# An attention and two expert layers: k's positions over 128 partitions for each head, and another order of the head

## The chip, the cores and the metric

One Trainium2 chip, one core. The metric is the device time of one execution in microseconds; the time of a kernel is the median of its runs.

## The reference

q, k and v are (4, 8, 576, 64): batch, heads, positions, width. q is made a softmax over its last axis, k a softmax over the *positions*; then `kv = k_s^T v` (64 by 64 for each head) and `attn = q_s kv`. The heads are laid side by side, which gives 2304 tokens of width 512. Two expert layers follow, each `x @ w_in` (512 to 2048), an activation (softplus in the first, ELU in the second) and `@ w_out` (2048 to 512):

```python
k_s = np.exp(k - np.max(k, axis=2, keepdims=True))
k_s = k_s / (np.sum(k_s, axis=2, keepdims=True) + 1e-09)
kv = np.einsum('bhsd,bhse->bhde', k_s, v)
x = np.einsum('bhsd,bhde->bhse', q_s, kv)   # then heads side by side, 2304 x 512
x = softplus(x @ w_in) @ w_out
x = elu(x @ w2_in) @ w2_out
```

## The kernel before, in words

The tokens are cut into six blocks of 384 (`t` = 0 to 5), worked on in three pairs. Each expert layer goes over the pairs, and for each pair over eight slices of 256 hidden columns ("quads"): the upward product (L833, with a seven-product scheme on halves; L895 in plain float32 for the first two quads of the first layer), the activation, the downward product (L1040, L1045, L1007, L1185). Weights arrive as raw words, are turned into float32 by ScalarE and VectorE (`add_words`, L662 to L687) and written back for later use.

**The head** is what runs before and beside the first of these. For q, `add_q` loads 384 rows, takes the softmax (VectorE, POOL or VectorE, ScalarE), transposes (L506), multiplies with the block-diagonal `kvbd` (L522) and copies the result to `sx` (L535), which is the input of the first layer. For k and v, `add_k(t, b, hps)` does one batch `b` and one or two pairs of heads `hps`: for batch 0 one pair in each of four steps, for batches 1, 2 and 3 two pairs in each of two steps. A pair puts head 0 on partitions 0 to 63 and head 1 on 64 to 127; each partition has nine positions of its head. In `add_k`, in order:

- L309 loads k, one DMA a pair, and L328 (batch 0, through `vr`, copied at L332) or L337 loads v, both on SP's queue. v has a column of ones beside it, for the sums.
- L346: VectorE takes the maximum over the nine positions of each partition, in four instructions.
- L354: TensorE transposes these maxima; L358: VectorE reduces them over a head's partitions.
- L366: TensorE spreads the maxima to the partitions, one matmul a head, into `pb`.
- L373: VectorE subtracts `pb` from k; L381: ScalarE takes exp.
- L390: TensorE adds up `kv` and the sums over positions into `pk`: for each of nine positions, two matmuls of 64 rows, one for each head, in two tiles of 64x64 of the array.
- L399, L403, L414 or L416: the sums become reciprocals, and the scaled `kv` goes into `kvbd`.

**What sets the order.** Every piece of work is a step with an engine, a cost, what it reads and writes, and for matmuls of the layers a due time. `Plan.order` (L59) works back from the due times to a latest start for each step, and then plays the engines forward: among the steps that can start at about the same time, the one with the earliest latest start goes first. A group of steps can be called more urgent by a number in `PRI` (L1366), which is taken off its latest starts: `k00` is the k steps of the first block that begin with pair 0, `q00` the q steps of the same, `k10` and `k12` those of the second block, `i0` and `o0` the words of the first slices of `w_in` and `w_out`, and so on. The order that comes out is written into the program once; each engine, and SP's queue of DMAs, works through its list in that order.

```python
@step(DMA, n * t_dma(P * C * D * 4), make=[...], after=LAT, behind=behind)          # k, L300
@step(DMA, t_dma(P * C * D * 4), make=[(vr, "xf")], after=LAT, behind=[kload[...]]) # v of batch 0, L325
@step(PE, 1.45 * n, r=[kk, vk], make=[(pk, bank(t))])                               # L383
def t_dma(n): return max(0.5, n / 300e3)                                            # LAT is 3.0 us
```

Of the kernel before, what the change touches and what calls it, by code (L numbers as in the profile page):

```python
# [8 lines left out]
F32 = mybir.dt.float32  # L9
# [3 lines left out]
ALU = mybir.AluOpType  # L13
AX = mybir.AxisListType

PE, ACT, DVE, POOL, DMA = "PE", "ACT", "DVE", "POOL", "DMA"
# [134 lines left out]
def t_dve(n, fast=False):  # L151
    return 0.069 + n / (1920 if fast else 960)
# [6 lines left out]
def t_dma(n):  # L159
    return max(0.5, n / 300e3)  # L160
# [3 lines left out]
def attention_moe_moe_kernel(  # L164
# [30 lines left out]
    nc = tc.nc  # L195
    B, H, S, D = q.shape
    NT, DM = out.shape
    DFF = w1_in.shape[1]
    P = 128
# [5 lines left out]
    NPAIR = NB // 2  # L205
    NP = H // 2
    C = S // 64
    EPS = 1e-9

    def pool(name, space=None, bufs=1):  # L210
# [8 lines left out]
        "g": (2, [P, 2 * BLK], F32), "gh": (3, [P, 2 * BLK], F32R), "gl": (3, [P, 2 * BLK], F32R),  # L219
        "s": (4, [P, BLK], F32), "xq": (2, [P, BLK], F32), "y": (2, [P, DM], F32), "yl": (2, [P, DM], F32),  # L220
        "k": (1, [P, 2 * C * D], F32), "v": (1, [P, 2 * C * (D + 1)], F32), "q": (1, [P, 2 * BLK], F32),
        "mx": (2, [P, 2 * D], F32), "mt": (1, [P, 8 * D], F32), "m": (4, [2 * D, 2], F32),
        "rs": (4, [P, 2], F32), "qm": (4, [P, 4 * R, 1], F32), "qd": (4, [P, 4 * R, 1], F32),
    }
    banks = {"ha": 2, "acc0": R, "acc1": R}
# [6 lines left out]
    T = {}  # L232

    def new(key, dt=None):
        ring = plan.tile_ring[key]
        _, shape, ring_dt = rings.get(ring, (0, [P, 512], F32))
        T[key] = pools[ring].tile(shape, dt or ring_dt, tag=ring, name="_".join(str(x) for x in key))
        return T[key]
# [28 lines left out]
    start, beside, now = {}, {}, 45.0  # L267
# [19 lines left out]
    def bank(t, rows=False):  # L287

        return "ha" if t > 1 else "acc0" if rows and not t else "acc1"

    def add_k(t, b, hps, behind=()):

        kk, vk, mx, pt, pb, pk, rs, m = (
            (s, b, hps[0]) for s in ("k", "v", "mx", "pt", "pb", "pk", "rs", "m")
        )
        n = len(hps)
        early = t == 0
        kt = lambda: T[kk][:, : n * C * D].rearrange("p (g c d) -> p g c d", g=n, d=D)
        vt = lambda: T[vk][:, : n * C * (D + 1)].rearrange("p (g c d) -> p g c d", g=n, d=D + 1)

        @step(
            DMA, n * t_dma(P * C * D * 4), make=[(kk, EARLY[0][hps[0]] if early else "k"), (vk, EARLY[1][hps[0]] if early else "v")],
            after=LAT, behind=behind,
        )
        def _():
            new(vk, F32)
            new(kk, F32)
            for g, hp in enumerate(hps):
                nc.sync.dma_start(  # L309
                    out=kt()[:, g],  # L310
                    in_=k[b, 2 * hp : 2 * hp + 2].rearrange("h (p c) d -> (h p) c d", c=C),
                )

        for hp in hps:
            kload[b, hp] = _

        @step(POOL, 0.05 * n, w=[vk])
        def _():
            nc.gpsimd.memset(vt()[:, :, :, D : D + 1], 1.0)

        vsrc = lambda hp: v[b, 2 * hp : 2 * hp + 2].rearrange("h (p c) d -> (h p) c d", c=C)
        if early:
            vr = ("vr", b, hps[0])

            @step(DMA, t_dma(P * C * D * 4), make=[(vr, "xf")], after=LAT, behind=[kload[b, hps[0]]])  # L325
            def _():
                T[vr] = new(vr, F32)[:, : C * D].rearrange("p (c d) -> p c d", c=C)
                nc.sync.dma_start(out=T[vr], in_=vsrc(hps[0]))  # L328

            @step(ACT, t_act(C * D), r=[vr], w=[vk])  # L330
            def _():
                nc.scalar.copy(vt()[:, 0, :, :D], T[vr])  # L332
        else:
            @step(DMA, n * t_dma(2 * P * C * D * 4), w=[vk], after=LAT)
            def _():
                for g, hp in enumerate(hps):
                    nc.sync.dma_start(out=vt()[:, g, :, :D], in_=vsrc(hp))  # L337

        mt = ("mt", b, hps[0])

        @step(DVE, sum(t_dve(n * x * D) for x in (4, 2, 1, 1)), r=[kk], make=[(mx, "mx"), (mt, "mt")])
        def _():
            half = new(mt)[:, : 4 * n * D].rearrange("p (g c d) -> p g c d", g=n, d=D)
            top = lambda o, x, y: nc.vector.tensor_tensor(o, x, y, op=ALU.max)  # L346
            top(half, kt()[:, :, :4], kt()[:, :, 4:8])
            top(half[:, :, :2], half[:, :, :2], half[:, :, 2:])
            top(half[:, :, 0], half[:, :, 0], half[:, :, 1])
            top(new(mx)[:, : n * D].rearrange("p (g d) -> p g d", g=n), half[:, :, 0], kt()[:, :, 8])  # L350

        @step(PE, 0.11, r=[mx], make=[(pt, bank(t))])
        def _():
            nc.tensor.transpose(new(pt)[: n * D, :P], T[mx][:, : n * D], ident)  # L354

        @step(DVE, t_dve(128), r=[pt], make=[(m, "m")])
        def _():
            nc.vector.tensor_reduce(  # L358
                new(m)[: n * D], T[pt][: n * D, :P].rearrange("d (h p) -> d h p", h=2), axis=AX.X, op=ALU.max
            )  # L360

        @step(PE, 0.12 * n, r=[m], make=[(pb, bank(t))])
        def _():
            p = new(pb)
            for j in range(2):
                nc.tensor.matmul(  # L366
                    p[64 * j : 64 * j + 64, : n * D], T[m][: n * D, j : j + 1].to_broadcast([n * D, 64]),
                    ident[: n * D, : n * D], start=True, stop=True,
                )

        @step(DVE, t_dve(n * C * D), r=[pb], w=[kk])
        def _():
            nc.vector.tensor_tensor(  # L373
                kt(), kt(),
                T[pb][:, : n * D].rearrange("p (g o d) -> p g o d", g=n, o=1).to_broadcast([P, n, C, D]),
                op=ALU.subtract,
            )

        @step(ACT, t_act(n * C * D), w=[kk], tab="exp")
        def _():  # L380
            nc.scalar.activation(kt(), kt(), AF.Exp)  # L381

        @step(PE, 1.45 * n, r=[kk, vk], make=[(pk, bank(t))])  # L383
        def _():
            p = new(pk)
            for g in range(n):
                for c in range(C):
                    for j in range(2):
                        rows = slice(64 * j, 64 * j + 64)
                        nc.tensor.matmul(  # L390
                            p[rows, g * (D + 1) : (g + 1) * (D + 1)], kt()[rows, g, c, :], vt()[rows, g, c, :],
                            start=(c == 0), stop=(c == C - 1),
                        )

        pkv = lambda: T[pk][:, : n * (D + 1)].rearrange("p (g d) -> p g d", g=n)

        @step(DVE, 0.07, r=[pk], make=[(rs, "rs")])
        def _():
            nc.vector.tensor_scalar(new(rs)[:, :n], pkv()[:, :, D], EPS, None, op0=ALU.add)  # L399

        @step(DVE, 0.075, w=[rs])
        def _():
            nc.vector.reciprocal(T[rs][:, :n], T[rs][:, :n])  # L403

        eng = DVE if early else ACT

        @step(eng, (0.28 if early else 0.5) * n, r=[pk, rs], w=[("kvbd", b % 2, hp) for hp in hps])
        def _():
            for g, hp in enumerate(hps):
                for j in range(2):  # L410
                    rows = slice(64 * j, 64 * j + 64)
                    o, i, f = kvbd[b % 2, hp][rows, rows], pkv()[rows, g, :D], T[rs][rows, g : g + 1]
                    if eng == DVE:
                        nc.vector.tensor_scalar(o, i, f, None, op0=ALU.mult)  # L414
                    else:
                        nc.scalar.activation(o, i, AF.Copy, scale=f)  # L416
# [868 lines left out]
    def add_store(m, p):  # L1285
# [55 lines left out]


    PRI = dict(
        k00=97, q00=38, k01=54, q01=13, k02=167, q02=154, k03=94, q03=54, k10=9, q10=83, k12=24, q12=11,
        k20=157, q20=11, k22=95, q22=30, k30=136, q30=45, k32=30, q32=0, x00=6, x01=36, x02=32, x10=48, x11=48,
        x12=213, y=59, w=-34, ahead=148, i0=-2, i1=43, i2=48, i3=173, i4=-23, i5=52, i6=66, i7=17, o0=105,
        o1=26, o2=29, o3=-28, o4=45, o5=18, o6=-2, o7=10,
    )

    def early(kind):  # L1350
# [23 lines left out]
    ahead = [(0, 1, 2), (0, 1, 4), (0, 1, 6), *((0, 2, f) for f in (0, 2, 3, 5, 6))]  # L1374
# [91 lines left out]
```

## Time and profile before

| | |
|---|---|
| median of 3 runs | 832.95 us (832.44 to 833.37) |
| the profiled execution, its own time | 833.62 us |
| its span, first to last instruction | 831.9 us, 13270 instructions |
| TensorE busy | 809.3 us, 97% |
| VectorE busy | 657.5 us, 79% |
| ScalarE busy | 564.7 us, 68% |
| DMA | 205.33 MB, mean 247 GB/s |

How to read it: a busy share is an average over the span, and the head and the layers have different limits. A matmul of float32 shows as two records. Lines are those of the kernel before; a group of instructions is named by what it writes and reads, with the shapes in partitions x elements.

### The profile page before, as it was taken

The page shows a single profiled execution, that of the slowest core. Times are in us where ns is not written, and L with a number is a line of the kernel's source. Part 1 is how long each engine was busy: PE and PEld are TensorE (multiplying, and loading weights), DVE is VectorE, ACT ScalarE, POOL GpSimd, SP SyncE. Part 2 cuts the span into 40 slices and gives each one's busy share as a digit, 9 for nine tenths or more (in the row PEclk, how much of TensorE's full clock was granted, in tenths as well). Part 3 has the DMA queues.
Part 4 walks back from the last instruction along what each step waited for, and adds up shares of the span by engine and source line. Part 5 has one row for each costly group of instructions (what it writes and reads, how often), then busy time and mean ns, then how long its engine had stood idle before and what let it go on. Part 6 is the DMA issues. An engine that isn't in the chain of part 4 may idle for free.

```text
span 831.9 us, 13270 instructions
## 1 busy us (share of the span) xinstructions
PE 809.3 (97%) x5110; PEld 732.4 (88%) x5110; DVE 657.5 (79%) x1088; ACT 564.7 (68%) x889; POOL 6.1 (1%) x28
## 2 busy tenths in 40 slices
PE   5799999999999999999999999999999999999997
PEld 4455788888889999999999998898999999999997
DVE  7879999979887768777679788968468697766775
ACT  4878987876787856756657767667466675557552
POOL 2000000000000000000000000000000000000000
PEclk9999999999999999999999999999999999999999
DMA  9597786636985556576855898987687676787563
GB/s 288 155 284 234 225 283 197 196 115 206 284 263 215 181 206 236 206 253 221 321 191 218 289 371 331 328 325 242 239 311 292 234 284 222 271 278 301 202 225 147
DMA packets 75166, 205.33 MB, mean 247 GB/s; under 512 B 18784, under 2 KB 34144, under 8 KB 65632
## 3 DMA queue, kind: packets, MB, share of 16 engines
q1 hardware_dynamic: 75104, 204.49, 71.0%
q8 instruction: 40, 0.66, 0.3%
q14 instruction: 22, 0.18, 0.1%
HBM read 143.65 MB, written 60.82 MB: 246 GB/s over the span
## 4 chain that ended last, share of the span: by engine, by line
PE 82%; DVE 8%; ACT 5%; DMA 2%; issue 2%; DVEq 0%; ACTq 0%; SPq 0%
PE ub L833 21%; PE acc L1007 15%; PE acc L1045 13%; PE uc L833 11%; PE Pb L1185 8%; PE ua L833 5%; PE Pc L1185 4%; PE Pa L1185 2%; PE px L522 1%; DMA wf_i<-wfd 1%; DVE mt L346 1%; PE acc L1040 1%; PE pk L390 1%; DMA raw_i<-in_moe_w_in_dram 1%; PE pq L506 1%
## 5 line engine op out<-in xcount | busy, mean ns | idle before, releaser
L833 PE MATMUL ub<-xf,wf_i 128*128 128x384 f32 x1104 | 226.5, 339 | 1.4 <-ACT s L846 1.1
L833 PEld LDWEIGHTS ub<-xf,wf_i 128*128 128x128 f32 x1104 | 189.3, 188 | 13.4 <-ACT s L846 4.3
L846 ACT COPY s<-ub 128x384 f32<-128x384 f32 x138 | 65.8, 477 | 72.7 <-PE ub L833 71.6
L833 PE MATMUL uc<-xf,wf_i 128*128 128x384 f32 x552 | 111.8, 337 | 0.7 <-ACT g L916 0.7
L1007 PE MATMUL acc<-gh,wo_o 128*128 128x512 f32 (+1 forms) x512 | 111.7, 340 | 0.0
L1045 PE MATMUL acc<-wo_o,gh 128*128 128x512 f32 x336 | 106.7, 398 | 0.0
L833 PEld LDWEIGHTS uc<-xf,wf_i 128*128 128x128 f32 x552 | 95.1, 188 | 5.7 <-ACT g L916 1.9
L867 DVE TENSOR_TENSOR h<-uc,s 128x384 f32<-128x384 f32 x92 | 51.1, 555 | 52.6 <-PE uc L833 47.5
L1007 PEld LDWEIGHTS acc<-gh,wo_o 128*128 128x128 f32 x512 | 82.9, 188 | 7.3
L1045 PEld LDWEIGHTS acc<-wo_o,gh 128*128 128x128 f32 x336 | 61.4, 188 | 9.0 <-ACT yt L1295 0.2
L1045 PE MATMUL acc<-wo_o,gl 128*128 128x512 f32 x168 | 66.5, 396 | 0.0
L1007 PE MATMUL acc<-gl,wo_o 128*128 128x512 f32 (+1 forms) x256 | 65.5, 336 | 0.0
L973 DVE TENSOR_TENSOR gl<-g,gh 128x768 fp32r<-128x768 f32 x60 | 57.2, 953 | 8.4 <-ACT gh L969 8.3
L833 PE MATMUL ua<-xf,wf_i 128*128 128x384 f32 x276 | 56.0, 337 | 0.0
L969 ACT CAST gh<-g 128x768 fp32r<-128x768 f32 x60 | 50.2, 836 | 7.1 <-DVE g L960 6.3
L833 PEld LDWEIGHTS ua<-xf,wf_i 128*128 128x128 f32 x276 | 47.9, 188 | 1.4 <-ACT sx L535 0.3
L746 DVE TENSOR_TENSOR wf_i<-st_i,wf_i 128x1024 fp32r<-128x1024 f32 x30 | 36.7, 1222 | 15.1 <-ACT wf_i L742 15.1
L1007 PEld LDWEIGHTS acc<-gl,wo_o 128*128 128x128 f32 x256 | 39.1, 188 | 5.3
L916 ACT ACTIVATE g<-h 128x384 f32<-128x384 f32 (+1 forms) x44 | 30.2, 686 | 16.3 <-DVE h L867 16.1
L1045 PEld LDWEIGHTS acc<-wo_o,gl 128*128 128x128 f32 x168 | 31.5, 187 | 6.8
L742 ACT CAST wf_i<-r_i 128x512 fp32r<-128x512 f32 (+1 forms) x48 | 23.2, 511 | 16.5 <-PE uc L833 16.4
L742 ACT CAST wf_i<-st_i 128x1024 fp32r<-128x1024 f32 x30 | 31.4, 1048 | 1.1 <-DVE st_i L726 1.0
(282 smaller groups left out, 1429.2 us busy)
## 6 DMA issues: line engine op xcount, KB each, us to landing
wf_i<-wfd SPq DMA_DIRECT2D x16, 1792.0 KB, 8.2
ws<-wos SPq DMA_DIRECT2D x28, 1024.0 KB, 5.4
raw_i<-in_moe_w_in_dram SPq DMA_DIRECT2D x16, 1024.0 KB, 6.5
raw_o<-in_moe_w_out_dram SPq DMA_DIRECT2D x16, 1024.0 KB, 7.4
wo_o<-wod SPq DMA_DIRECT2D x14, 1024.0 KB, 5.5
wfd<-wf_i SPq DMA_DIRECT2D x8, 1792.0 KB, 7.8
r_i<-w32i SPq DMA_DIRECT2D x24, 512.0 KB, 6.0
wod<-wo_o SPq DMA_DIRECT2D x8, 1024.0 KB, 5.2
```

Source lines behind the costliest of these rows:

```text
L346: top = lambda o, x, y: nc.vector.tensor_tensor(o, x, y, op=ALU.max)
L742: nc.scalar.copy(view(0, lo, n, c), get())
L746: nc.vector.tensor_tensor(view(1, lo, n, c), get(), view(0, lo, n, c).bitcast(F32), op=ALU.subtract)
L833: nc.tensor.matmul(ps[:, :BLK], T[wk][:, lo : lo + P], T[xk][:, (2 * c + kc) * BLK : (2 * c + kc + 1) * BLK], start=(i in first and kc == ...
L846: nc.scalar.copy(new(sk), T[key][:, :BLK])
L867: nc.vector.tensor_tensor(T[hk][:, half * BLK : (half + 1) * BLK], T[key][:, :BLK], T[sk], op=ALU.add)
L916: nc.scalar.activation(o, i, AF.Softplus)
L969: nc.scalar.copy(new(hk), T[gk])
L973: nc.vector.tensor_tensor(new(lk), T[gk], T[hk].bitcast(F32), op=ALU.subtract)
L1007: nc.tensor.matmul(ps, T[wk][:, lo : lo + P], T[g][:, cols], start=(first and n == 0 and starts), stop=(f == NQ - 1 and j == 1 and n == 2) ...
L1045: nc.tensor.matmul(ps, T[g][:, col : col + P], T[wk][:, (2 * a + j) * DM : (2 * a + j + 1) * DM], start=(first and n == 0), stop=(f == NQ ...
L1185: nc.tensor.matmul(ps[:, x * 256 : x * 256 + 256], T[fk][a][:, r * P : (r + 1) * P], T[ck][:, q * 512 + b * 256 : q * 512 + b * 256 + 256] ...
```

## The change

For each head, positions 0 to 511 are laid over all 128 partitions, four positions each, and the last 64 positions over the 64 partitions of that head, one each. A pair of heads has the same nine columns of 64 as before: four of head 0, four of head 1, and one that both share, half by half. A load becomes four DMAs. The maxima keep their four instructions for one pair but go pair by pair for two; transposing is one matmul for each pair, the spreading three, the subtraction two instructions for one pair and three for two. The product of k and v has eight matmuls of 128 rows (into 64 rows of output each) and two of 64, in place of eighteen of 64. The costs of three steps in the plan are set anew; those of the loads stay. All numbers of `PRI` are replaced.

```diff
-        "mx": (2, [P, 2 * D], F32), ... "m": (4, [2 * D, 2], F32),
+        "mx": (2, [P, 4 * D], F32), ... "m": (4, [P, 2], F32),
+        def load(dst, src, hp):
+            for h in range(2):
+                nc.sync.dma_start(
+                    out=dst[:, W * h : W * h + W], in_=src[b, 2 * hp + h, : P * W].rearrange("(p c) d -> p c d", c=W)
+                )
+            for h in range(2):
+                rows = slice(64 * h, 64 * h + 64)
+                nc.sync.dma_start(out=dst[rows, 2 * W], in_=src[b, 2 * hp + h, P * W :])
...
-                nc.sync.dma_start(
-                    out=kt()[:, g],
-                    in_=k[b, 2 * hp : 2 * hp + 2].rearrange("h (p c) d -> (h p) c d", c=C),
-                )
+                load(kt()[:, g], k, hp)
...
-            top(half, kt()[:, :, :4], kt()[:, :, 4:8])
-            top(half[:, :, :2], half[:, :, :2], half[:, :, 2:])
-            top(half[:, :, 0], half[:, :, 0], half[:, :, 1])
-            top(new(mx)[:, : n * D].rearrange("p (g d) -> p g d", g=n), half[:, :, 0], kt()[:, :, 8])
+            for g in range(n):
+                whole = kt()[:, g, : 2 * W].rearrange("p (h c) d -> p h (c d)", h=2)
+                top(half[:, g].rearrange("p (h c) d -> p h (c d)", h=2), whole[:, :, : 2 * D], whole[:, :, 2 * D :])
+                two = half[:, g].rearrange("p (h c) d -> p h c d", h=2)
+                top(most[:, g], two[:, :, 0], two[:, :, 1])
+            for h in range(2):
+                rows = slice(64 * h, 64 * h + 64)
+                top(most[rows, :, h], most[rows, :, h], kt()[rows, :, 2 * W])
...
-            for j in range(2):
-                nc.tensor.matmul(
-                    p[64 * j : 64 * j + 64, : n * D], T[m][: n * D, j : j + 1].to_broadcast([n * D, 64]),
-                    ident[: n * D, : n * D], start=True, stop=True,
-                )
+            for g in range(n):
+                of = lambda cols: T[m][:, g : g + 1].to_broadcast([P, cols])
+                lo = g * 3 * D
+                nc.tensor.matmul(p[:, lo : lo + P], of(P), ident, start=True, stop=True)
+                for h in range(2):
+                    nc.tensor.matmul(
+                        p[64 * h : 64 * h + 64, lo + P : lo + P + D], of(64), ident[:, 64 * h : 64 * h + 64], ...
+                    )
...
-        @step(PE, 1.45 * n, r=[kk, vk], make=[(pk, bank(t))])
+        @step(PE, 0.75 * n, r=[kk, vk], make=[(pk, bank(t))])
...
-                for c in range(C):
+                for c in range(W + 1):
                     for j in range(2):
                         rows = slice(64 * j, 64 * j + 64)
+                        src, at = (slice(0, P), j * W + c) if c < W else (rows, 2 * W)
                         nc.tensor.matmul(
-                            p[rows, ...], kt()[rows, g, c, :], vt()[rows, g, c, :],
-                            start=(c == 0), stop=(c == C - 1),
+                            p[rows, ...], kt()[src, g, at, :], vt()[src, g, at, :],
+                            start=(c == 0), stop=(c == W),
                         )
...
-        k00=97, q00=38, k01=54, q01=13, k02=167, q02=154, k03=94, q03=54, k10=9, q10=83, k12=24, q12=11,
-        k20=157, q20=11, k22=95, q22=30, k30=136, q30=45, k32=30, q32=0, x00=6, x01=36, x02=32, x10=48, x11=48,
-        x12=213, y=59, w=-34, ahead=148, i0=-2, i1=43, i2=48, i3=173, i4=-23, i5=52, i6=66, i7=17, o0=105,
-        o1=26, o2=29, o3=-28, o4=45, o5=18, o6=-2, o7=10,
+        k00=25, q00=150.5, k01=151.5, q01=-8, k02=31.5, q02=24.5, k03=104, q03=3.5, k10=7.5, q10=87, k12=8, q12=-9,
+        k20=55.5, q20=15, k22=39.5, q22=61, k30=113.5, q30=360, k32=90, q32=9, x00=-8, x01=-43.5, x02=118, x10=82.5,
+        x11=25, x12=155.5, y=41, w=11, ahead=28, i0=-14.5, i1=37, i2=83.5, i3=276, i4=28.5, i5=-21.5, i6=106,
+        i7=155.5, o0=44.5, o1=32.5, o2=202.5, o3=-25.5, o4=182.5, o5=153, o6=-258.5, o7=55,
```

(W is 4, C is 9, D is 64, P is 128; `n` is the number of pairs in the step, `g` counts them.)

## Rows read from the trace of the kernel before

**Rows 1.** The page: the span, and each engine's busy time, share, instructions.

```profile
span 831.9 us, 13270 instructions
...
PE 809.3 (97%) x5110; PEld 732.4 (88%) x5110; DVE 657.5 (79%) x1088; ACT 564.7 (68%) x889; POOL 6.1 (1%) x28
```

**Rows 2.** Busy by stretch: stretch, length, PE, PEld, DVE, ACT, POOL, clock, DMA share, GB/s.

```profile
3.70:26.00 22.30, 15.26 (x184) 10.57 (x184) 21.23 (x64) 9.47 (x17) 3.31 (x4) 0.93 0.94 281
...
60.00:80.00 20.00, 19.77 (x70) 11.75 (x69) 19.79 (x28) 16.16 (x21) 0.00 (x0) 1.00 0.77 235
...
100.00:120.00 20.00, 20.00 (x100) 17.81 (x100) 20.00 (x31) 16.36 (x23) 0.00 (x0) 1.00 0.81 276
```

**Rows 3.** The chain of waits in order of time: start, length, what; "x" counts records.

```profile
0.73 2.98 DMA k<-in_k_dram
...
11.96 4.15 PE pk L390 x72
...
69.22 0.61 DVE mt L346
...
135.28 0.11 PE pt L354
...
136.78 0.37 PE pb L366 x4
...
216.68 2.25 PE pk L390 x72
```

**Rows 4.** SP's queue in order of time, 0 to 60 us: start, length, DMAs issued.

```profile
0.73 2.76 SPq L309 DMA_DIRECT2D k<-in_k_dram  x6
3.54 0.43 SPq L328 DMA_DIRECT2D vr<-in_v_dram  x1
...
14.40 0.60 SPq L646 DMA_DIRECT2D raw_i<-in_moe_w_in_dram  x1
```

**Rows 5.** Groups by line and shape, 0 to 60 us: busy us, mean ns.

```profile
L373 DVE TENSOR_TENSOR k<-k,pb 128x576 f32<-128x576 f32 x4 | 2.9, 746 | 0.0
...
L373 DVE TENSOR_TENSOR k<-k,pb 128x1152 f32<-128x1152 f32 x2 | 2.7, 1350 | 1.5 <-PE pb L366 1.5
...
L346 DVE TENSOR_TENSOR mt<-mt 128x128 f32<-128x128 f32 x6 | 1.8, 292 | 0.2
...
L346 DVE TENSOR_TENSOR mt<-k 128x256 f32<-128x256 f32 x4 | 1.7, 416 | 3.8 <-DMA k<-in_k_dram 3.7
...
L346 DVE TENSOR_TENSOR mt<-k 128x512 f32<-128x512 f32 x2 | 1.4, 678 | 0.0
...
L366 PE MATMUL pb<-ident,m 128*64 128x128 f32 x8 | 0.9, 298 | 0.5 <-DVE m L358 0.5
L346 DVE TENSOR_TENSOR mx<-mt,k 128x64 f32<-128x64 f32 x4 | 0.9, 224 | 0.1
...
L346 DVE TENSOR_TENSOR mt<-mt 128x256 f32<-128x256 f32 x2 | 0.9, 426 | 0.1
...
L358 DVE TENSOR_REDUCE m<-pt 128x2 f32<-128x128 f32 x2 | 0.6, 288 | 0.0
```

**Rows 6.** All engines in order of time, 0 to 62 us: start, length, engine, line, instructions.

```profile
22.13 0.44 PE L366 MATMUL pb<-ident,m 128*64 128x128 f32 x4 [0.49 <-DVE m L358]
...
27.75 1.14 ACT L662 ACTIVATE raw_i<-raw_i 128x1024 f32<-128x1024 f32 x1
...
34.29 5.32 PE L895 MATMUL up<-sx,w_ti_i 128*128 128x384 f32 x16
```

**Rows 7.** DMA issues, 0 to 60 us: count, KB each, median us from issue to landing.

```profile
raw_i<-in_moe_w_in_dram SPq DMA_DIRECT2D x3, 1024.0 KB, 6.3
```

More of the change, by code (lines that the diff above doesn't have):

```diff
@@ L207, in attention_moe_moe_kernel @@
     C = S // 64
+    W = S // P
     EPS = 1e-9
@@ L221, in attention_moe_moe_kernel @@
         "k": (1, [P, 2 * C * D], F32), "v": (1, [P, 2 * C * (D + 1)], F32), "q": (1, [P, 2 * BLK], F32),
-        "mx": (2, [P, 2 * D], F32), "mt": (1, [P, 8 * D], F32), "m": (4, [2 * D, 2], F32),
+        "mx": (2, [P, 4 * D], F32), "mt": (1, [P, 8 * D], F32), "m": (4, [P, 2], F32),
         "rs": (4, [P, 2], F32), "qm": (4, [P, 4 * R, 1], F32), "qd": (4, [P, 4 * R, 1], F32),
@@ L319, in _ @@
             nc.gpsimd.memset(vt()[:, :, :, D : D + 1], 1.0)
-        vsrc = lambda hp: v[b, 2 * hp : 2 * hp + 2].rearrange("h (p c) d -> (h p) c d", c=C)
         if early:
@@ L327, in _ @@
                 T[vr] = new(vr, F32)[:, : C * D].rearrange("p (c d) -> p c d", c=C)
-                nc.sync.dma_start(out=T[vr], in_=vsrc(hps[0]))
+                load(T[vr], v, hps[0])
             @step(ACT, t_act(C * D), r=[vr], w=[vk])
@@ L336, in _ @@
                 for g, hp in enumerate(hps):
-                    nc.sync.dma_start(out=vt()[:, g, :, :D], in_=vsrc(hp))
+                    load(vt()[:, g, :, :D], v, hp)
         mt = ("mt", b, hps[0])
-        @step(DVE, sum(t_dve(n * x * D) for x in (4, 2, 1, 1)), r=[kk], make=[(mx, "mx"), (mt, "mt")])
+        @step(DVE, t_dve(n * 4 * D) + t_dve(n * 2 * D) + 2 * t_dve(n * D), r=[kk], make=[(mx, "mx"), (mt, "mt")])
         def _():
+            top = lambda o, x, y: nc.vector.tensor_tensor(o, x, y, op=ALU.max)
@@ L345, in _ @@
             half = new(mt)[:, : 4 * n * D].rearrange("p (g c d) -> p g c d", g=n, d=D)
-            top = lambda o, x, y: nc.vector.tensor_tensor(o, x, y, op=ALU.max)
-            top(half, kt()[:, :, :4], kt()[:, :, 4:8])
-            top(half[:, :, :2], half[:, :, :2], half[:, :, 2:])
-            top(half[:, :, 0], half[:, :, 0], half[:, :, 1])
-            top(new(mx)[:, : n * D].rearrange("p (g d) -> p g d", g=n), half[:, :, 0], kt()[:, :, 8])
-        @step(PE, 0.11, r=[mx], make=[(pt, bank(t))])
+            most = new(mx)[:, : 2 * n * D].rearrange("p (g h d) -> p g h d", g=n, h=2)
@@ new lines, in _ @@
+            for g in range(n):
+                whole = kt()[:, g, : 2 * W].rearrange("p (h c) d -> p h (c d)", h=2)
+                top(
+                    half[:, g].rearrange("p (h c) d -> p h (c d)", h=2), whole[:, :, : 2 * D], whole[:, :, 2 * D :]
+                )
[4 more added lines that the diff above has]
+                top(most[rows, :, h], most[rows, :, h], kt()[rows, :, 2 * W])
@@ L353, in _ @@
+        @step(PE, 0.11 * n, r=[mx], make=[(pt, bank(t))])
         def _():
-            nc.tensor.transpose(new(pt)[: n * D, :P], T[mx][:, : n * D], ident)
-        @step(DVE, t_dve(128), r=[pt], make=[(m, "m")])
+            p = new(pt)
+            for g in range(n):
+                nc.tensor.transpose(p[:, g * P : g * P + P], T[mx][:, g * P : g * P + P], ident)
+        @step(DVE, t_dve(128 * n), r=[pt], make=[(m, "m")])
         def _():
             nc.vector.tensor_reduce(
-                new(m)[: n * D], T[pt][: n * D, :P].rearrange("d (h p) -> d h p", h=2), axis=AX.X, op=ALU.max
+                new(m)[:, :n], T[pt][:, : n * P].rearrange("d (g p) -> d g p", g=n), axis=AX.X, op=ALU.max
@@ L360, in _ @@
             )
-        @step(PE, 0.12 * n, r=[m], make=[(pb, bank(t))])
+        @step(PE, 0.35 * n, r=[m], make=[(pb, bank(t))])
         def _():
             p = new(pb)
-            for j in range(2):
-                nc.tensor.matmul(
-                    p[64 * j : 64 * j + 64, : n * D], T[m][: n * D, j : j + 1].to_broadcast([n * D, 64]),
-                    ident[: n * D, : n * D], start=True, stop=True,
-                )
[L371 to L376, printed above, removed]
-            )
+            for g in range(n):
+                of = lambda cols: T[m][:, g : g + 1].to_broadcast([P, cols])
[3 more added lines that the diff above has]
+                    nc.tensor.matmul(
+                        p[64 * h : 64 * h + 64, lo + P : lo + P + D], of(64), ident[:, 64 * h : 64 * h + 64],
+                        start=True, stop=True,
+                    )
@@ new lines, in _ @@
+        @step(DVE, n * t_dve(8 * D) + t_dve(n * D), r=[pb], w=[kk])
+        def _():
+            most = T[pb][:, : n * 3 * D].rearrange("p (g i d) -> p g i d", g=n, i=3)
+            less = lambda o, y: nc.vector.tensor_tensor(o, o, y, op=ALU.subtract)
+            for g in range(n):
+                less(
+                    kt()[:, g, : 2 * W].rearrange("p (h c) d -> p h c d", h=2),
+                    most[:, g, :2].rearrange("p h (o d) -> p h o d", o=1).to_broadcast([P, 2, W, D]),
+                )
+            less(kt()[:, :, 2 * W], most[:, :, 2])
@@ L386, in _ @@
             for g in range(n):
-                for c in range(C):
+                for c in range(W + 1):
                     for j in range(2):
                         rows = slice(64 * j, 64 * j + 64)
+                        src, at = (slice(0, P), j * W + c) if c < W else (rows, 2 * W)
                         nc.tensor.matmul(
-                            p[rows, g * (D + 1) : (g + 1) * (D + 1)], kt()[rows, g, c, :], vt()[rows, g, c, :],
-                            start=(c == 0), stop=(c == C - 1),
+                            p[rows, g * (D + 1) : (g + 1) * (D + 1)], kt()[src, g, at, :], vt()[src, g, at, :],
+                            start=(c == 0), stop=(c == W),
                         )
```

## The prediction

> **What bounds the kernel now.** I read the page first: TensorE is busy for 97% of the span, VectorE for 79% [rows 1]. That average hides two regimes, so the table by stretches comes next. From 100 us on TensorE is full (20.00 of 20) and whatever shortens its own work shortens the run. Before that VectorE is the fuller engine: 21.23 of 22.30 us from 3.70 to 26.00, 19.79 of 20 from 60 to 80, where TensorE shows as busy but is often waiting for a VectorE result [rows 2]. The chain of waits says the same by name. It opens with the first load of k, runs over VectorE pieces with one long TensorE piece (the product of k and v, 4.15 us at 11.96), and still passes through VectorE at 69.22; from 135 on the steps on k stand in it as TensorE pieces [rows 3]. So one microsecond added to VectorE before some 80 us counts nearly whole, one saved on TensorE counts only after that, and the head also hangs on when its loads are issued.
>
> **TensorE.** A step on k is done four times for one pair of heads (batch 0) and six times for two pairs: two for batch 1 before 50 us, four for batches 2 and 3, the last three of them where TensorE is the chain. On the chain such a two-pair step costs 0.11 (transposing the maxima) + 0.37 (spreading them) + 2.25 (72 records of the product) = 2.73 us [rows 3]. The product is 18 matmuls a pair, two records each; the change makes it 10, so 40 records a step. At the same 31.25 ns a record (2.25/72) that is 1.25 us. One transpose becomes two: 0.22. The spreading was two matmuls of 64 output rows side by side over 128 columns; it becomes, per pair, one full one of 128 columns (two records, at the 0.11 of the transpose: 0.22) and two half ones of 64 columns (half of 0.37: 0.19), 0.81 a step. After: 2.28 us, 0.45 less. I take 0.4, for three steps: **-1.2 us**. The price of the 31.25 ns is not certain: the pairs of 64x64 tiles run side by side now, the new ones are 128 rows by 64 columns. The nearest row is the spreading, in 128*64 tiles: its four records end 0.44 us after the first began, at 0.298 us each, so they start 0.05 us apart [rows 5, 6], less than half of the 0.11 that a 128-column record takes alone [rows 3]. Side by side is therefore the better reading, and 62.5 ns a record (2.50 us a step) the other bound.
>
> A rule speaks against this part. The Trainium skill (TensorEngine Tiling (Array Packing), section Tiling Modes, Key Properties) says that a change of tiling mode, not merely of tile, drains the engine. By it the new step, which alternates between 128x64 and 64x64 for every pair and between full and half width in the spreading, would drain at some five places more; no row here isolates that.
>
> **VectorE.** The maxima of one pair take 0.416 + 0.292 + 0.224 + 0.224 now; the new four instructions have 256, 128 and twice 64 elements: the same. The subtraction (0.746 for 576 elements) splits into 512 (0.746 x 512/576 = 0.66) and 64 (0.22): +0.14, four times +0.56. A two-pair step goes from 0.678 + 0.426 + 2 x 0.292 = 1.69 to 2 x 0.416 + 4 x 0.292 = 2.00 for the maxima (+0.31), from 0.288 to about 0.43 for the reduction over 256 (+0.14), from 1.35 to 2 x 0.66 + 0.29 = 1.61 for the subtraction (+0.26): +0.71 [rows 5]. Batch 0 and the first step of batch 1 lie ahead of the first matmul of the first expert layer at 34.29 [rows 6], with VectorE 95% busy: 0.56 + 0.71 = +1.3. The second step of batch 1 and the first of batch 2 lie where the chain still crosses VectorE; the chain shows the maxima there (0.61 at 69.22), less surely the rest, so I count the maxima alone: 2 x 0.31 = **+0.6**, with 0 and 1.4 as bounds. The last three steps cost VectorE 2.1 us more that TensorE's full queue hides; without that cover they would cost it.
>
> **Loads.** Each load of k or v for a pair turns from one DMA into four. SP issues one after another: six loads of k take it 2.76 us, 0.46 each, whatever lies in them (1024 KB of raw weights 0.60 with the wait, one of v 0.43) [rows 4]. First effect: the first pair of k is complete when its fourth DMA lands, issued 3 x 0.46 = 1.4 us later than its only one was. The first two maxima need only the two wide DMAs, one issue later (0.46), and last 0.416 + 0.292 = 0.7 us [rows 5]; the third needs the last DMA. So the delay lies between 0.5 and 1.4, and I take 1.4 - 0.7 = 0.7. VectorE's way to the first matmul is then 1.3 + 0.7 = 2.0 us longer.
>
> Second effect: the queue behind them. The planner still charges a load as before, and it sets the loads of v behind those of k by its 3 us latency, so four pairs of k of batch 0 (16 issues) and two of batch 1 (8) go out before the first v, then 16 of v, four of q, eight of batch 1's v, and then the raw words of w_in: the new priority of i0 (-14.5 for -2) doesn't move it ahead. That is 52 issues: 0.73 + 52 x 0.46 = 24.7 us in place of 14.40 [rows 4]. Landing takes 6.3 us [rows 7]: 31.0, where ScalarE took the words at 27.75 and TensorE its first matmul 6.5 us after [rows 6]: 37.5, or 3.2 us late. At 0.40 us an issue it would be 27.8, and nothing is late. So the head is late by the larger of 2.0 and something between 0 and 3.2: I take **+2.5**, bounds 1.0 and 3.5.
>
> **The new order** moves priorities alone. No row prices it; the nearest is the 8 issues of batch 1's k ahead of the first v, 8 x 0.46 = 3.7 us, which an order may win or lose. I take 0, between the two, and leave both ends to the range.
>
> **Sum.** +2.5 + 0.6 - 1.2 = +1.9 us. The profiled execution took 833.62 (span 831.9 and 1.7 around it), 0.7 above the median of 832.95; against the median 834.9. About 0.2%, 1.7 us, is what a measurement of this kernel can tell from no change.
>
> **The rivals.** *Faster: the product is the head's own chain.* From 11.96 to 16.11 the chain is TensorE in 72 records of 57.6 ns, nearly twice the 31.25 of later ones [rows 3]; 40 in their place save 32 x 57.6 ns = 1.85 us. If the order brings v and q forward by those 8 issues, VectorE starts on the results that much sooner, its 1.3 us are paid from that, and the end is 1.3 - 1.85 - 1.0 (the next product, 72 records to 40 at 31.25 ns) - 1.2 = -2.75: 830.2. It decides if the first product starts by 13 us. For it: 4.15 us in one piece on the chain; against: VectorE is busy at 95% meanwhile. Chance 0.33.
>
> *No difference.* An issue costs nearer 0.40 us, the head is late by 1.3 and the later VectorE work is absorbed: +1.3 - 1.2 = +0.1, 833.0. For it: the raw words lay 7 us before use (14.40 + 6.3 = 20.7 against 27.75) [rows 4, 6, 7]. Chance 0.20.
>
> *The product gains nothing.* Halves of columns don't overlap, or the array empties between tile shapes: 62.5 ns a record makes a step 0.22 + 0.81 + 2.50 = 3.53, +0.8 for three steps, +2.4, and the sum 2.5 + 0.6 + 2.4 = +5.5: 838.5. The change then doesn't do what it says. Against it stands the 0.05 us between records in 128*64 tiles. Chance 0.07. The skill's rule on draining, named above, is the second of its two causes.
>
> **How the numbers follow.** My forecast has 0.40 and a range of its own of 834.0 to 837.0 (head 1.6 to 3.5, the rest as summed, and 0.7 for the order). It and the last rival are slower by over 0.2%, though the forecast only just: together 0.47. Same has 0.20, faster 0.33. For 8 times in 10 the range must hold forecast, no difference and most of the faster case, whose own spread is the 1 us by which the order may do better: 829.2 to 838.0.
>
> **What would show it.** Right: ten matmuls a pair at near 31 ns a record in the steps after 130 us, each two-pair step near 2.3 us on the chain; VectorE busy some 5 us more in all (0.56 + 6 x 0.71); SP issuing without a break to about 24 us; the first matmul of the expert layer near 36.8. Wrong: that matmul at 34 or earlier (the order gave it back), raw words issued before 17 us, or records at 50 ns and more. If the head is on time and the end is still late, the loss lies with VectorE between 60 and 140 us.

## The result, and the profile after

| | before | after |
|---|---|---|
| median | 833.16 us (832.44 to 833.55, 4 runs) | 845.05 us (844.18 to 845.30, 4 runs) |
| ratio, 95% interval | | 1.0142 [1.0124, 1.0159] |
| profiled execution, span | 833.62, 831.9 us | 844.95, 843.2 us |
| first matmul of the first expert layer | 34.29 us | 44.78 us |
| from there to the end of the span | 797.6 us | 798.4 us |

Slower by 11.9 us; 834.9 was predicted, and 838.0 was the upper end. The last two rows divide the loss: 10.5 of the 11.3 us of span are lost before the first matmul of the expert layer, 0.8 behind it. (The lower row has to be read with care: a head that runs late has done other work meanwhile, which then lies no longer behind it.)

The page of the kernel after, its span, its busy times and the first line of its chain by engine; the first two answer to [rows 1]:

```profile
span 843.2 us, 13082 instructions
...
PE 815.9 (97%) x4916; PEld 737.5 (87%) x4916; DVE 662.0 (79%) x1116; ACT 566.8 (67%) x891; POOL 6.1 (1%) x28
...
PE 91%; SPq 3%; ACT 2%; DVE 2%; DMA 1%; issue 1%; DVEq 0%; ACTq 0%
```

Two things stand out. TensorE has 194 records fewer and yet 6.6 us more of busy time. And SP's queue has 3% of the chain, some 25 us. The stretches of [rows 2] show where, in the kernel after (stretch, length, PE, PEld, DVE, ACT, POOL, clock, DMA share, GB/s):

```profile
3.70:26.00 22.30, 11.53 (x90) 8.01 (x90) 12.58 (x44) 5.09 (x9) 1.66 (x2) 1.00 0.50 139
60.00:80.00 20.00, 20.00 (x103) 12.50 (x103) 16.09 (x26) 15.79 (x26) 0.13 (x1) 1.00 0.83 288
100.00:120.00 20.00, 20.00 (x130) 15.91 (x129) 19.27 (x37) 16.06 (x25) 0.13 (x1) 1.00 0.68 195
```

In the head nothing is full any more: VectorE has fallen from 21.23 of 22.30 us to 12.58, and the 16 DMA engines are half idle (0.50, 139 GB/s; 0.94 and 281 before). What fills the time is the issuing of DMAs. This is SP's queue of the kernel after in order of time (start, length, DMAs issued), to be held against [rows 4]:

```profile
0.73 0.87 SPq L304 DMA_DIRECT2D k<-in_k_dram  x2
1.65 1.20 SPq L309 DMA_DIRECT2D k<-in_k_dram  x2
...
14.17 1.06 SPq L304 DMA_DIRECT2D vr<-in_v_dram  x2
...
27.50 2.02 SPq L304 DMA_DIRECT2D v<-in_v_dram  x2
...
31.50 0.48 SPq L669 DMA_DIRECT2D raw_i<-in_moe_w_in_dram  x1
```

The first v goes out at 14.17 (3.54 before), the raw words at 31.50 (14.40 before). Between 0.73 and 31.50 stand the 52 issues that the prediction counted, so one takes 30.77 / 52 = 0.59 us. The chain of waits of the kernel after, in order of time, is SP alone until 23.55, in pieces that alternate between some 0.45 and 0.59, and then:

```profile
23.08 0.47 SPq L309
...
23.59 2.21 DMA vr<-in_v_dram
...
26.64 1.55 PE pk L413 x20
28.19 0.72 PE pb L383 x2
...
33.29 1.62 PE px L545 x2
...
35.55 2.95 PE pk L413 x40
...
86.06 0.22 PE pb L383 x2
86.29 0.26 PE pb L385 x4
86.55 0.42 PE pb L383 x2
86.97 0.27 PE pb L385 x4
93.99 1.76 PE pk L413 x40
```

The last v of batch 0 waits for its place in SP's queue; its product, the spreading for batch 1 and batch 1's product follow on TensorE. Beside this, in order of time on all engines (start, length, engine, line, and in brackets the idle time and its releaser), the raw words go their way to the matmul at 44.78; before, these were at 27.75 and 34.29 [rows 6]:

```profile
37.96 1.14 ACT L685 ACTIVATE raw_i<-raw_i 128x1024 f32<-128x1024 f32 x1 [1.47 <-DMA raw_i<-in_moe_w_in_dram]
...
40.62 1.27 ACT L439 ACTIVATE kvbd<-pk,rs 64x64 f32<-64x64 f32 x4
...
41.91 1.19 ACT L699 ACTIVATE raw_i<-raw_i 128x1024 uint32<-128x1024 uint32 x1
...
44.74 0.30 PEld L918 LDWEIGHTS up<-sx,w_ti_i 128*128 128x128 f32 x2 [0.41 <-DVE w_ti_i L710]
44.78 1.65 PE L918 MATMUL up<-sx,w_ti_i 128*128 128x384 f32 x4
```

The two ways meet on ScalarE: the second conversion of the words (L699) comes in its list behind `kvbd` (L439), which needs batch 1's product, and the first matmul waits for what VectorE makes of that conversion (`w_ti_i`).

### The profile page after: what moved, and what is told of

It is laid out like the page before. It is cut to its first block, busy times and chain, and to the rows that moved or that the text cites. A ratio compares the mean times of both kernels' runs of the same rounds, so it can differ in the third digit from the quotient of the medians.

```text
span 843.2 us, 13082 instructions
## 1 busy us (share of the span) xinstructions
PE 815.9 (97%) x4916; PEld 737.5 (87%) x4916; DVE 662.0 (79%) x1116; ACT 566.8 (67%) x891; POOL 6.1 (1%) x28
## 4 chain that ended last, share of the span: by engine, by line
PE 91%; SPq 3%; ACT 2%; DVE 2%; DMA 1%; issue 1%; DVEq 0%; ACTq 0%
PE ub L856 22%; PE acc L1030 16%; PE acc L1068 13%; PE uc L856 11%; PE Pb L1208 8%; PE ua L856 5%; PE Pc L1208 4%; PE acc L1063 2%; PE Pa L1208 2%; PE px L545 2%; PE up L918 2%; PE pk L413 2%; SPq L309 1%; SPq L304 1%; PE pq L529 1%; DMA r_i<-w32i 1%
## 5 line engine op out<-in xcount | busy, mean ns | idle before, releaser
L939 ACT ACTIVATE g<-h 128x384 f32<-128x384 f32 (+1 forms) x44 | 30.2, 687 | 10.7 <-DVE h L890 10.5
```

The source lines that it names most:

```text
L939: nc.scalar.activation(o, i, AF.Softplus)
```

## The experiments

Theory A: the loss is the issues, four times as many, that SP puts out ahead of what the head waits for. Rival B: the loss is the new product and its spreading on TensorE, by the shapes of their tiles. Rival C: it is the new order. "Head" is the start of the first expert-layer matmul, "rest" the span minus it; both are of the profiled execution, which lies up to 1.9 us from the median (844.05 in e5), so that a difference of less than 2 us in the rest says little by itself. A ratio is to the kernel before measured beside the run (833.16 for the kernel after, 832.6 to 833.6 for the others).

| run | time | ratio [95%] | raw words issued | head | rest |
|---|---|---|---|---|---|
| after | 845.05 | 1.0142 | 31.50 | 44.78 | 798.4 |
| e1_before_four_dmas | 843.76 | 1.0117 [1.0102, 1.0133] | 29.24 | 42.74 | 800.7 |
| e2_after_old_order | 857.94 | 1.0295 [1.0261, 1.0330] | 32.98 | 47.12 | 809.5 |
| e3_before_new_order | 851.84 | 1.0209 [1.0191, 1.0227] | 12.46 | 33.88 | 816.8 |
| e4_after_two_dmas | 839.65 | 1.0067 [1.0052, 1.0082] | 22.85 | 39.19 | 798.2 |
| e5_after_grouped | 842.19 | 1.0111 [1.0097, 1.0125] | 31.53 | 44.34 | 798.0 |
| e6_after_v_on_act | 843.91 | 1.0130 [1.0116, 1.0144] | 24.49 | 42.76 | 799.2 |
| e7_two_grouped_act | 840.27 | 1.0086 [1.0072, 1.0100] | 20.68 | 42.60 | 795.0 |
| e8_after_raw_first | 888.07 | 1.0657 [1.0642, 1.0671] | 0.74 | 53.30 | 832.8 |
| e9_two_grouped_full | 835.89 | 1.0041 [1.0028, 1.0054] | 22.57 | 37.91 | 795.0 |
| e10_full_new_plan | 834.00 | 1.0006 [0.9997, 1.0015] | 23.99 | 39.97 | 792.1 |
| e11_full_new_plan_2 | 839.64 | 1.0074 [1.0062, 1.0087] | 19.39 | 40.21 | 797.3 |
| e12_before_new_plan | 831.95 | 0.9978 [0.9968, 0.9989] | 12.38 | 32.77 | 796.3 |

### The issues alone, in the old layout

The kernel before, with nothing changed but that each load of k or v is cut into four DMAs of 32 partitions:

```diff
+        def load(dst, src, hp):
+            for j in range(4):
+                s0 = 32 * C * (j % 2)
+                nc.sync.dma_start(
+                    out=dst[32 * j : 32 * j + 32],
+                    in_=src[b, 2 * hp + j // 2, s0 : s0 + 32 * C].rearrange("(p c) d -> p c d", c=C),
+                )
```

> The kernel before, with each load of k and v cut into four DMAs of 32 partitions; layout, arithmetic, order and the size of a contiguous piece stay. My theory, that SP's time to issue is what the change costs: the raw words of w_in go out at 28 to 32 us in place of 14.4, the first matmul of the expert layer begins at 42 to 46, the time is 8 to 12 us over the kernel before. Rival one, the new order of the head does the harm: no change (within 1.5 us). Rival two, the new layout's work on VectorE and TensorE does it: no change either.

Measured 10.2 us over the kernel before (833.6 beside it). Its SP queue, and below it its first expert-layer matmul on TensorE:

```profile
0.73 11.07 SPq L304 DMA_DIRECT2D k<-in_k_dram  x24
...
29.24 0.60 SPq L651 DMA_DIRECT2D raw_i<-in_moe_w_in_dram  x1
```

```profile
42.74 5.32 PE L900 MATMUL up<-sx,w_ti_i 128*128 128x384 f32 x16
```

The same bytes, matmuls and VectorE work, with only the DMAs cut, lose nearly all that the change loses. The six pairs of k take 11.07 us to issue in place of 2.76 [rows 4], 0.46 each as before; the rest of the queue up to the raw words takes longer an issue (0.62). This is in the old layout and order; what the issues cost in the new ones, e4 below tells more nearly.

### The order alone, both ways

The kernel after with the old `PRI` (e2), and the kernel before with the new one (e3).

> The changed kernel with the priorities of the kernel before. Issue theory: as many DMAs stand ahead of the raw words, so 842 to 847 us. Rival one, the order: 833 to 836 us. Rival two, the layout's work: about 845 us.

> The kernel before with the new priorities alone. Issue theory: 26 issues in the head as before, so within 2 us of 833. Rival one, the order: 841 to 846 us. Rival two, the layout's work: within 2 us of 833.

Both were far off. The new order is worth 12.9 us to the new layout (857.94 to 845.05), and the old layout loses 18.2 us by it (851.84 against 833.6), though its head is on time (33.88). The waits of TensorE, first in e2 from 47 to 100 us, then in e3 from 100 to 240 us (engine, line, releaser: us in total, times, longest):

```profile
PE up L918 <- ACT g L939: 8.5, 2, 6.6
```

```profile
PE uc L833 <- DVE h L867: 3.4, 2, 2.0
PE ua L833 <- ACT kvbd L416: 3.2, 1, 3.2
```

In e2 TensorE waits 8.5 us for ScalarE's activations; in the kernel after that wait isn't there. In e3 it waits 3.2 us for `kvbd`, which stands on ScalarE behind two conversions of `raw_o`, as the chain of that run shows. These waits are not all of e3's 18.2 us: TensorE's busy time grows by 7.9 us too (817.2 against 809.3). Part of that is the clock: the wait for `kvbd` leaves TensorE with 0.18 us of work in 3.40, and right behind it the granted clock reads 0.50, the level of 1.2 GHz (e3; stretch, length, PE, clock, DMA share, GB/s):

```profile
101.00:104.40 3.40, 0.18 (x1) 0.98 0.86 281
104.40:106.00 1.60, 1.58 (x5) 0.50 0.94 279
```

So an order that is written out once holds for the durations it was made for. Rival C falls in its plain form, in which e2 would have taken 833 to 836 us. Order and layout don't add up: under the old order the new layout is 24.3 us slower than the old one (857.94 to 833.6), under the new order it is 6.8 faster (845.05 to 851.84).

### Fewer issues in the new layout

Both heads of a pair in one DMA where the access allows it: two DMAs a load for k and batch 0's v, three for the later v. 30 issues go out ahead of the raw words in place of 52.

```diff
-            for h in range(2):
-                nc.sync.dma_start(out=dst[:, W * h : W * h + W], ...)
-            for h in range(2):
-                rows = slice(64 * h, 64 * h + 64)
-                nc.sync.dma_start(out=dst[rows, 2 * W], in_=src[b, 2 * hp + h, P * W :])
+            nc.sync.dma_start(out=dst[:, : 2 * W].rearrange("p (h c) d -> p h c d", c=W), ...)
+            nc.sync.dma_start(out=dst[:, 2 * W], in_=src[b, 2 * hp : 2 * hp + 2, P * W :])
```

> The changed kernel with a load of k and of batch 0's v in two DMAs (both heads' wide part, both heads' rest) and one of the other v in three, the same bytes in the same pieces. Issue theory: some 30 issues ahead of the raw words in place of 52, at 0.57 us, so these go out near 18 us, the first matmul of the expert layer begins at 36 to 39, and the time is 835 to 839 us. Rivals one and two: still near 845 us, since order and arithmetic are the changed kernel's.

5.4 us faster than the kernel after, head 5.6 earlier, rest as it was: A again. It missed what was expected, closely in the time (839.65 for 835 to 839) and by more in the words (22.85 for 18), since 30 issues take 22.11 us, 0.74 each. A DMA for both heads can take longer to issue: the wide ones of k and batch 0's v take 0.43 to 1.36 us, 0.79 on average (SP's queue of this run; the first is a wide one):

```profile
4.48 1.36 SPq L304 DMA_DIRECT2D k<-in_k_dram  x1
5.88 0.52 SPq L308 DMA_DIRECT2D k<-in_k_dram  x1
...
22.85 1.10 SPq L668 DMA_DIRECT2D raw_i<-in_moe_w_in_dram  x1
```

### The shapes of tiles

All matmuls of a step with one tile shape together, in the spreading and in the product; their number is the same (the start flag of a product goes with its first pair alone).

```diff
-            for g in range(n):
-                for c in range(W + 1):
+            for c0, c1 in ((0, W), (W, W + 1)):
+              for g in range(n):
+                for c in range(c0, c1):
...
```

> The changed kernel with the matmuls of a step on two pairs grouped by the shape of their tiles: in the spreading both full ones first and then the four halves, in the product all of 128 rows first and then the four of 64. Same matmuls. If changes of tile shape cost, a two-pair step on the chain, 3.40 us now (0.27 + 1.37 + 1.76), falls by two changes in the spreading's and two in the product's part, to 2.8 to 3.1 us, and five steps give 1.5 to 3 us: 842 to 843.5. If the halves simply run at their pace and changes are free: 3.40 us again and 845 us. The issue theory says nothing on it; the first matmul of the expert layer stays at 44 to 46.

2.9 us faster than the kernel after by the medians, with the head 0.4 earlier. The chain of this run, a spreading (the full matmuls, then the halves) and the product of a two-pair step twice:

```profile
257.59 0.44 PE pb L382 x4
258.03 0.38 PE pb L387 x8
...
265.95 1.46 PE pk L416 x40
286.91 1.46 PE pk L416 x40
```

Forty records take 1.46 us in place of 1.76, the spreading 0.82 in place of 1.17; the whole step (0.22 for the transposes) 2.50 where at least 2.8 was expected. Of B this much is shown: going to and fro between tile shapes costs some 0.3 us a two-pair product and as much a spreading. Grouped, a record still takes 36.5 ns, not 31.25.

### The words first, and v from another queue

In e8 `i0` is set to 200, so that the raw words are SP's first DMA; in e6 batch 0's v is issued from ScalarE's queue.

```diff
-... i0=-14.5, ...
+... i0=200, ...
```

> The changed kernel with one priority changed, i0 = 200, which puts the raw words of the first slice ahead of all loads; the planner re-orders what follows. If the raw words alone hold the first matmul of the expert layer (the step that the prediction took): it begins at 34 to 38 us. If every load in the queue does, the last q among them, which now stands behind 47 issues: 41 to 46 us, and 842 to 850 us in the end, the order after it being another.

```diff
-                load(T[vr], v, hps[0])
+                load(T[vr], v, hps[0], q=nc.scalar)
```

> The changed kernel with the 16 DMAs of batch 0's v issued from ScalarE's queue. Issue theory: 36 issues are left on SP ahead of the raw words, which go out at 20 to 23 us in place of 31.5; the first matmul of the expert layer begins at 35 to 39 and the time is 836 to 840 us. Rival, that the loads are slow in the transfer itself (more and smaller pieces) and not in the issue: as many pieces are moved, so within 2 us of 845.

Both missed. With the words at 0.74 the head ends at 53.30 and the whole takes 888: the words are not all that the head waits for. In the order that the planner then makes, batch 1's v goes out from 32.29 to 37.5 (24.86 to 30.83 in the kernel after), and its product begins at 43.13 (35.48). The rest is 34 us longer as well; TensorE waits there for ScalarE and VectorE, as in e2 and e3 (the longest wait is 4.5 us), and the whole of it was not traced.

With v on ScalarE's queue SP comes to the words 7 us earlier, yet the head gains 2.0, and 843.91 lies in the range of that run's rival, slow transfers. Against this rival stands e1, which lost 10.2 us with pieces of the old size. The chain of e6 shows what the head hung on (start, length, what):

```profile
15.86 4.17 DMA q<-in_q_dram
...
23.92 0.53 ACT q L490
...
24.60 1.55 PE pk L413 x20
```

A load of q, its softmax, and then the last product of batch 0, at 24.60 in place of 26.64: 2.0 us earlier, as the head. From there to the first expert-layer matmul it is 18.16 us, and 18.14 in the kernel after. In all six kernels with this order (the kernel after, e4 to e7, e9) that stretch takes 16.8 to 18.2 us, while from the issue of the words it is 12.8 to 21.9. So the head follows batch 0's v at least as much as the words. What the issues cost on ScalarE, its list in order of time shows (engine and line; its own queue is ACTq):

```profile
1.67 2.97 ACTq L309 DMA_DIRECT2D vr<-in_v_dram  x2
...
11.34 2.10 ACTq L304 DMA_DIRECT2D vr<-in_v_dram  x2
13.97 1.64 ACTq L309 DMA_DIRECT2D vr<-in_v_dram  x2
15.66 0.68 ACT L403 ACTIVATE k<-k 128x576 f32<-128x576 f32 x1 [3.78 <-DVE mx L351]
```

A pair of issues takes 0.9 to 3.0 us there, the eight pairs 12.8 us in place of 8.5 on SP, and the later ones stand between the exps, which come at their set place in the list. The Trainium skill (DMA: Bandwidth & Descriptors, section Rules for kernel authors) says that spreading DMAs over issuing engines saves only sequencer issue time; by these rows SP's time was saved and more than that paid on ScalarE.

### What the new layout can do

e7 is e4, e5 and v on ScalarE's queue together. e9 is e4 and e5 with the spreading by its full matmul alone: the halves are left out, and the subtraction takes the shared column from the full one, in two VectorE instructions.

```diff
-                for h in range(2):
-                    nc.tensor.matmul(p[64 * h : 64 * h + 64, lo + P : lo + P + D], of(64), ident[...], ...)
...
-            less(kt()[:, :, 2 * W], most[:, :, 2])
+            for h in range(2):
+                rows = slice(64 * h, 64 * h + 64)
+                less(kt()[rows, :, 2 * W], most[rows, :, h])
```

> The changed kernel with all three: two DMAs a load (three for the later v), batch 0's v from ScalarE's queue, matmuls grouped by tile shape. Issue theory: 22 issues ahead of the raw words on SP, fewer than the 26 of the kernel before; the first matmul of the expert layer at 33 to 36 us, and with what grouping gives 830 to 834 us, so about the kernel before or under it. If transfers or the layout's work bound the head: 837 us and more.

> The changed kernel with two DMAs a load, the matmuls grouped by tile shape, and the spreading by its full matmul alone: the subtraction of the shared column reads the two halves of that one, in two instructions on VectorE in place of one, and the four half matmuls of a step on two pairs are gone. All loads on SP, the plan's costs and so the order as changed. If TensorE's added pieces (the spreading 1.37 us for 0.37 on the chain, and nearly double while it runs at the lower pace) are what is left of the loss beside the issues: the first matmul of the expert layer begins 1 to 3 us before the 39.2 of the kernel with two DMAs alone, and the time is 834 to 837 us, against 839.65. If only the issues count: 39 and 839 to 840.

e7 missed: words out at 20.68, but the head at 42.60, so again the other queue bought nothing; batch 0's last product begins at 25.54, where e4 without that queue has it at 21.49. (Its expectation held 22 issues against 26 in the kernel before; ahead of the words that kernel has 18 [rows 4].) e9 came as expected, 3.8 us below e4. Its rest is 2.6 us shorter than before (795.0 to 797.6), its head 3.6 longer; its profiled execution is 0.9 under its median. On its chain the spreading takes mostly 0.44 and the product 1.46: with 0.22 for the transposes some 2.1 us a two-pair step, below the 2.73 of before. The product of 128 rows does gain on TensorE, once tile shapes are grouped and the half matmuls are gone; what remains is the head. The chain of e9, the words in the head first and then a later step:

```profile
22.57 8.92 DMA raw_i<-in_moe_w_in_dram
31.51 1.16 ACT raw_i L682
...
250.54 0.44 PE pb L380 x4
...
258.51 1.46 PE pk L410 x40
```

Last, orders made for costs from these traces. e10 and e11 are e9 with 1.2 us a load and 0.24 us a spreading in the plan, TensorE early on at 1.8 times its cost (before 30 us, in e12 before 18), and two new sets of `PRI`; e12 is the layout of before with the early factor and a new `PRI`, its loads as before.

```diff
-PE_EARLY = 1.1
+PE_EARLY = 1.8
...
-            DMA, n * t_dma(P * C * D * 4), ...
+            DMA, n * 1.2, ...
```

> The kernel of the run before (two DMAs a load, grouped, spreading by the full matmul) with the plan's costs set to what the traces show (1.2 us for a load of k or of batch 0's v, the spreading and the subtraction, TensorE's lower pace early on) and the priorities looked for again with these. If the head is still late because the order was made for loads that cost less than they do: the raw words land before they are wanted, the first matmul of the expert layer begins at 33 to 36 us, and with the 795.0 us that the kernel before this one takes from there on, 829 to 833 us. If the layout itself holds the head back: 835 us or more, whatever the order.

> The same kernel with another order, from a second search that began at the changed kernel's priorities. As the run beside it: 829 to 834 us if order and issue are what is left, 835 or more if it is the layout. The spread between the two shows what one search is worth.

> The kernel before, its layout and its single DMAs, with an order looked for again in the same way: what a new search alone gives. If new orders are worth some us by themselves: 828 to 832 us. If the old order was as good as this can find: 832 to 836.

e10 is not to be told from the kernel before (1.0006, twelve runs against 23). It lies between its two expected ranges, and its gain is not where it was looked for: the head is at 39.97, not at 33 to 36, and the rest is the shortest of all (792.1). e11 is 5.6 us slower than e10 by its order alone, although its 839.64 lies in the range that was given for the layout. e12, the layout of before, is the fastest and just inside the first of its ranges: 831.95, 0.2% below the kernel before (its interval ends at 0.9989). In its profiled execution, 1.0 under its median, the head ends 1.5 us earlier and the rest is 1.3 shorter.

Step by step the new layout went from 845.05 to 839.65 with fewer issues (e4), to 835.89 with the tile shapes put right (e9), to 834.00 with another order (e10); the old layout with an order looked for in the same way took 831.95. So the new layout is not shown to win. Two orders of one kernel are 5.6 us apart, so the last 2 us don't decide between the layouts either.

## Why the prediction was wrong

The direction was right, and so was the cause named first, issues ahead in SP's queue; the size was not, nor the path taken to it: +1.9 us was forecast and +11.9 came.

**The price of an issue is the step that failed.** The count (52), the order of the queue, the landing and the time after it were right: the words reach ScalarE 6.46 us after their issue began (6.3 said), and the first matmul starts 6.82 us after that (6.5 said). But 0.46 us an issue came from six loads of k at the opening of the queue [rows 4]; it was 0.59 on the average of 52, so 24.7 became 31.50. These 6.8 us, 0.16 of landing and 0.3 behind it put the first matmul at 44.78 and not at 37.5. On top the head was entered at +2.5 where its own working gave 3.2.

**Its bound failed too.** The lower end, 0.40, was tried; no upper end was. The rows held one: before, the raw words went out at 14.40 behind 18 issues, 0.76 us each [rows 4]. That figure includes waits, but it is an end, and by it the words would have gone out at 0.73 + 52 x 0.76 = 40 us. With it the range would have held the result.

**The path was too short.** The prediction let the head hang on VectorE or on the raw words. A third way ends beside the words in the kernel after: the last v of batch 0, 42 issues deep, its product at 26.64, batch 1's step and `kvbd`, behind which ScalarE makes the second conversion of the words (41.91). In e6 and e7 the words went out 7.0 and 10.8 us earlier, and the head gained 2.0 and 2.2. So it is partly luck that the time behind the words came out as said. An estimate from these rows: at 0.46 us an issue the last v would be out by 0.73 + 42 x 0.46 = 20.05 in place of 24.19, and with as much behind it the head would end at 40.6. Of the 7.3 us between 37.5 and 44.78 some 4 are then the price and some 3 this path.

**VectorE's way in the head (+1.3 and +0.7)** did not decide. VectorE's total rose by 4.5 us, as the prediction's "some 5" had it. But the first maxima start earlier, not later: the first 256 columns land at 3.33 us in the kernel after, while a pair's whole k landed at 3.71 before [rows 3]. And with a pair of k every 2.3 us (four issues) VectorE waits: 12.58 busy of 22.30. The prediction took the larger of two ways, which was the right form with one way left out.

**VectorE behind the head (+0.6)** is not seen. The maxima of batch 1's second step have 1.44 us of the chain of the kernel after (1.72 before), those of batch 2's first step none. From 52.99 to 110 us the chain of the kernel after is TensorE alone, and from 60 to 80 VectorE is busy for 16.09 of 20 us, where it was for 19.79.

**TensorE (-1.2)** has the wrong sign. A two-pair step on the chain costs 0.27 + 1.17 + 1.76 = 3.20 us (the last five lines of the chain above, and 0.27 for the transposes), where 2.28 was said and 2.73 was before; three such steps are +1.4 us. (The 2.73 takes the smallest of three transposes; the others stand in the chain of before with 0.30 and 0.33, so +1.4 is an upper end.) Two terms were mis-sized. The spreading takes 1.17 (0.22 + 0.26 + 0.42 + 0.27) where 0.22 + 0.19 a pair, 0.81 in all, was said. A record of the product takes 44 ns, between the 31.25 taken and the bound of 62.5. So the rival that the product gains nothing (3.53 a step) was nearer on this term, but it had the head at +2.5 and so 838.5. The Trainium skill (TensorEngine Tiling (Array Packing), section Tiling Modes, Key Properties) names the cause of a part, the drain at a change of tiling mode; the trace of e5 agrees, with 1.76 to 1.46 us in the product and 1.17 to 0.82 in the spreading when most changes were taken away.

**The faster rival** needed the first product to start by 13 us. It started at 18.59 in the kernel after, with four pairs of k and two of batch 1's ahead of the first v. Its saving is there in part: the product of a pair takes 1.55 us there in place of half of 4.15 [rows 3].

**The order (0, within 3.7)** can't be priced alone, as e2 and e3 show. The bound, drawn from eight issues, was too small, and the wrong kind: the waits that an order makes or spares lie on ScalarE and VectorE, tens of microseconds later.

Open: why an issue took 0.59 us and not 0.46. Pieces of 0.43 and of 0.59 alternate in the kernel after for both shapes of load, so neither the bytes nor the partitions of a DMA alone explain it. Nor is 0.59 one price: the 24 issues of k took 0.56 each, the eight of batch 1's v 0.75 (24.86 to 30.83). Why the raw words of e9 take 8.92 us from issue to landing, in place of 6.3 [rows 7], is open too.

## What to carry to other kernels

A DMA that is cut costs an issue each time, and the price is paid by whatever stands behind it in the queue, not by the data that was cut; count the issues ahead of each load that the first heavy stage needs, not of one alone, and price them by an average over a long run of that queue. Take an upper end for that price from the same queue, waits included. When a layout changes the durations, an order written out by hand has to be made again before the layout can be judged; and keep matmuls of one tile shape together.

## What was not expected of the hardware

The issuing queue can bound a kernel while the DMA engines are half idle: 0.50 busy, 139 GB/s, from 3.70 to 26.00. The granted clock reads 1.00, the level of 2.4 GHz, in that stretch of the kernel after, where before it read 0.93 [rows 2]; yet TensorE's records in the head take 1.7 to 1.8 times as long as later ones (20 of the product 1.55 us at 26.64, 40 of them 1.76 at 93.99; the same two records of `px` 1.62 us at 33.29 and 0.93 at 44.03). TensorE had been idle for much of the stretch ahead of these. What sets that pace was not tried.
